# Attention, gated and softplus layers on one core: an operand sum moved into its PSUM bank

## The chip, the cores and the metric

One core of one Trainium2 chip runs the whole kernel as one program. The metric is device time in microseconds; a run's time is that of its one core. Before the change the median of 3 runs is 587.61 us (587.58 to 587.76).

## What is computed

The reference is attention with a learned distance bias, then a gated layer, then a softplus layer, all in fp32:

```python
scores = scale * q @ k.T + bias(heads, S, S)         # B=2, H=8, S=576, D=64
attn = softmax(scores) ; out = attn @ v               # -> x: 1152 tokens x 512
x = (silu(x @ w_gate) * (x @ w_val)) @ w_out          # 512 -> 1536 -> 512
x = softplus(x @ w_in) @ w_out2                       # 512 -> 2048 -> 512
```

The products of the layers take fp32 operands as two parts each: a high part (a rounded cast) and a low part (the value minus its high part). They also use a scheme with fewer products of 2 x 2 blocks (Strassen's, in Winograd's form). The attention output, turned so that features lie on partitions, is the right operand. Its four blocks are called B11, B12, B21 and B22, and the scheme needs sums of them: T1 = B12 - B11, T2 = B22 - T1, T3 = B22 - B12, T4 = T2 - B21 up to sign. Each sum must exist as a high part and a low part before the gated layer starts at about 186 us.

## The kernel before, in words

The attention stage is written out slot by slot. A unit is a pair of heads of one batch; `UNITS` (L495) lists eight of them. Each unit is done in two halves of its rows: sub 0 has 4 chunks and 256 columns, sub 1 has 5 chunks (one of them, "mix", takes both heads) and 320 columns. `run_slot` (L521) handles one chunk, and PE, VectorE (DVE), ScalarE (ACT), GpSimd (POOL) and SP each execute in the order in which this code issues, since the whole stage stands under a manual schedule (L594). In a slot the order is:

1. the chunk's scores on PE (L333, into `ps`, of which there are two buffers),
2. for a half whose value products ended in the slot before, `finish` (L440) is made, a generator whose steps are spread over slots; in the code before it is only appended here (L553 to L557),
3. `gather` (L408): copies of transposed weights from PSUM, mostly on ACT,
4. `biased` (L342, DVE L354): scores plus bias into SBUF and the row minimum; it frees `ps`,
5. `softmax` (L366) of the chunk before: exp on ACT (L368), and at the end of a batch a reduce and a reciprocal on DVE (L372, L375) and scalings on POOL (L378),
6. two steps of `prep`: high parts of the next unit's k and q on DVE or ACT (L189, L191), low parts on POOL or DVE (L195). One of four low parts of k is DVE's, three are POOL's,
7. `advance(late)` (L568): the next step of each `finish`,
8. transposes on PE (L405) and, when a half's last piece is gathered, all its value products (L432) into `po`, a PSUM bank of which there is one. Then `advance(waiting)` (L586) runs the steps that waited for the next half's products.

So a score buffer is free for the scores of chunk n+2 when `biased` of chunk n is done. "The first chunk behind" a half's products is called n1 below, the next ones n2, n3 and so on.

The name B12 is reached four times: in units 1 and 3, in both halves. Called **A** (unit 1, sub 0), **B** (unit 1, sub 1), **C** (unit 3, sub 0) and **D** (unit 3, sub 1) here, their products end at about 72.9, 92.4, 114.6 and 123.6 us. Before, `finish` does there (L462 to L473): in n1's step 7 an ACT copy `po` to `b12` and DVE `t1f = po - B11h`; at the end of the next half's products DVE `t1f -= B11l` (SBUF); one slot later ACT T1h, a cast of `t1f`; at the end of the products behind that (one half later still for sub 1) DVE T1l = `t1f` - T1h (SBUF). `t1f` and `b12` lie in a dead part of `bias1`, so the trace calls them bias. All subtractions of `minus` show as line L452. Units 4 and 5 make B22 and read `t1f` and `b12` (L474 to L478).

Of the kernel before, what the change touches and what calls it, by code (L numbers as in the profile page):

```python
# [44 lines left out]
BLOCK = "block"  # L45
# [58 lines left out]
def tile_kernel(ctx: ExitStack, tc, qT, kT, vS, vT, wg, wv, wo, wi, wo2, table, out):  # L104
    nc = tc.nc
# [11 lines left out]
    def slots(pool, tag, names):  # L117

        for name in names:
            n = len([1 for t in SLOTS.values() if t[0] == tag])  # L120
            SLOTS[name] = (tag, [pool.tile([P, 2, S], F32R, tag=f"{tag}{2 * n + i}", name=f"{name}{t}") for i, t in enumerate("hl")])

    def opener(stack):
        return lambda name, bufs, **k: stack.enter_context(
            tc.tile_pool(name=name, bufs=bufs, reuse_waits="tile", **k)
        )

    rctx = ExitStack()
    with ExitStack() as actx:
# [38 lines left out]
        def load_k(i):  # L168
            pr, b = UNITS[i]
            kr = kp.tile([P, 2, S], F32, tag="kst", name="kr") if i < PLAIN else bias[0][:, :2]  # L170
            load(kr, kT, pr, b)
            return dict(i=i, pr=pr, b=b, kr=kr)

        def load_q(u):
            u["qr"] = early[7] if u["i"] == 1 else qraw.tile([P, 2, S], F32, tag="qr", name="qr")
            load(u["qr"], qT, u["pr"], u["b"])

        def load_v(u):
            pr, b = u["pr"], u["b"]
            v = u["v"] = vp.tile([P, 4, 3 * D], F32, name="v")  # L180
            vt = u["vt"] = vts[u["i"] % 3]
            sp.dma_start(out=v, in_=vS[b, pr].rearrange("p (c e) -> p c e", c=4))
            thirds = lambda ap: ap.rearrange("p (t e) -> p t e", t=3)
            sp.dma_start(out=thirds(vt[:D])[:, ::2], in_=thirds(vT[b, pr])[:, ::2])
            sp.dma_start(out=vt[D:, D : 2 * D], in_=vT[b, pr, :, D : 2 * D])
# [254 lines left out]
        def finish(u):  # L440

            if u["i"] == 2 and u["sub"] == 0:
                slots(xp, "a", ("B21", "B22"))
            if u["i"] == 4 and u["sub"] == 0:
                right.close()
                SLOTS["rp8"] = (None, opener(rctx)("rp8", 1, side="right"))
                slots(SLOTS["rp8"][1], "r", ("T2", "T3", "T4"))
            pr, sub, po = u["pr"], u["sub"], u["po"]
            n = 320 if sub else 256
            cols = slice(256 * sub, 256 * sub + n)  # L450
            po = po[:, :n]
            minus = lambda o, a, b, eng=nc.vector: eng.tensor_tensor(o, a, b, op=ALU.subtract)  # L452
            at = lambda name: [t[:, pr % 2, cols] for t in SLOTS[name][1]]
            floats = lambda name: [t.bitcast(F32) for t in at(name)]
            name = f"B{1 + pr // 2}{1 + u['b']}"
            if name != "B12":
                nc.scalar.copy(at(name)[0], po)
            k = pr % 2
            home = bias[1][:, 2 * k : 2 * k + 2, cols]
            t1f, b12 = home[:, 0], home[:, 1]  # L460
            chains = []
            if name == "B12":  # L462
                nc.scalar.copy(b12, po)
                minus(t1f, po, floats("B11")[0])
                yield BLOCK
                minus(t1f, t1f, floats("B11")[1])
                yield
                nc.scalar.copy(at("T1")[0], t1f)
                yield BLOCK
                if sub:  # L470
                    yield BLOCK
                minus(at("T1")[1], t1f, floats("T1")[0])
                return  # L473
            elif name == "B22":  # L474
                t2, t3 = t2f[:, k, cols], tmpp.tile([P, 320], F32, name="t")[:, :n]
                minus(t2, po, t1f)
                minus(t3, po, b12)
                chains = [("T2", t2), ("T3", t3)]  # L478
            elif name == "B21":
                t4 = tmpp.tile([P, 320], F32, name="t")[:, :n]  # L480
                minus(t4, po, t2f[:, k, cols])
                chains = [("T4", t4)]
            if not u["eager"]:
                yield
            if name != "B12":
                minus(at(name)[1], po, floats(name)[0])
            if u["eager"]:
                yield
                yield
            for to, t in chains:  # L490
                nc.scalar.copy(at(to)[0], t)
                yield
                minus(at(to)[1], t, floats(to)[0], nc.vector if u["eager"] else nc.gpsimd)
# [27 lines left out]
        def run_slot():  # L521
            nonlocal turned, done, prep, before, slot
            if slot < len(chunks):
                i, sub, n = chunks[slot]
                if n == 0:
                    for _ in prep:
                        pass
                    if (i, sub) == (1, 0):
                        load_v(units[1])
                    elif (i, sub) == (0, 1):  # L530
                        units.append(load_k(2))
                    elif sub and i + 1 < 2 * NP:
                        load_q(units[i + 1])
                        if i > 1:
                            load_v(units[i + 1])
                        prep = itertools.chain(prepare_k(units[i + 1]), prepare_q(units[i + 1], 0))
                    elif i > 1 and not sub:
                        if i + 1 < 2 * NP:
                            units.append(load_k(i + 1))
                        if i == 2:  # L540
                            load_v(units[2])
                            units[2][0].update(v=units[2]["v"], vt=units[2]["vt"])
                        prep = prepare_q(units[i], 1)
                    if i < PLAIN:
                        job(units[i], sub)
                    if i == NP and sub == 0:
                        flat = lambda ap: ap.rearrange("p a s -> p (a s)")
                        pairs[2:] = [flat(bias[c][:, 2 * a : 2 * a + 2]) for a in range(2) for c in (2, 3)]
                        mixes[1] = flat(bias[4][:, :2])[:, : 5 * P]
                        nc.gpsimd.memset(mixes[1][:, S:], 0.0)  # L550
                u = units[i][sub]
                got = scores(u, n)
            for w in done:  # L553
                w["eager"] = slot >= len(chunks) - 1
                late.append(finish(w))
                if w["eager"]:
                    next(late[-1])  # L557
            done = []
            for w, piece, got_t in turned:
                gather(w, piece, *got_t)  # L560
            if slot < len(chunks):
                biased(u, n, *got)
            if before:
                softmax(*before)
                before = None
            for _ in range(2):
                next(prep, None)
            advance(late)  # L568
            held, turned = [t[:2] for t in turned], []

            over = slot >= len(chunks)
            for _ in range(2 if slot % 9 in TWICE or over else 1):
                if jobs and jobs[0][2] <= slot:
                    w, piece, _ = jobs.pop(0)
                    turned.append([w, piece, transposes(w, piece, over and (piece == "f" or next(spare)))])
            gathered.extend(held)

            ends = [i + 1 for i, (w, piece) in enumerate(gathered) if piece == PIECES[w["sub"]][-1]]
            last_job = over and gathered and gathered[0][0] is units[-1][1]
            for _ in range(len(gathered) if last_job else max(ends, default=0)):  # L580
                w, piece = gathered.pop(0)
                values(w, piece)
                if piece == PIECES[w["sub"]][-1]:
                    done.append(w)
            if done:
                advance(waiting)  # L586
            if slot < len(chunks):
                before = (u, n)
                if n == 3 + sub:
                    jobs.extend((u, piece, slot + LAG) for piece in PIECES[sub])  # L590
            slot += 1
# [125 lines left out]
    class Quad:  # L717
# [8 lines left out]
        def floats(self):  # L726
            self.x = as_float(self.n)
# [129 lines left out]
    with tc.manual_schedule(engines={E.PE}):  # L857
# [118 lines left out]
        for m, order in ((2, (0, 1, 2)), (3, (2, 0, 1))):  # L976
            pt = [wide()[:, 0] for _ in TB]
            for fbs in [order[:1], order[1:]] if m == 3 else [(fb,) for fb in order]:
                at = {fb: blocks.index((m, fb)) for fb in fbs}
                ws = {fb: convert(NL1 + 3 + i // 2)[i % 2] for fb, i in at.items()}  # L980
                for ps, (o, n) in reversed(list(zip(pt, TB))):
                    for fb in fbs:
                        part = lambda k: [g[NK * fb + k][:, o : o + n] for g in (gh, gl)]
# [167 lines left out]
```

## Time and profile before

| | us |
|---|---|
| median of 3 runs (lowest, highest) | 587.61 (587.58, 587.76) |
| profiled execution: span from first to last instruction | 585.8 |
| median less span (what lies around the span) | 1.8 |
| attention stage behind the bias, its value products and sums | about 63 to 186 |
| PE, DVE, ACT, POOL busy in the span | 575.7, 454.2, 374.8, 98.4 |

The page has no time of the profiled execution beyond its span; the 1.8 us is the difference to the median of the runs shown. PE's granted clock is at its upper level in every slice. A busy PE is not PE at its peak, since the ends of matmuls are modelled, so the distance between the same two steps of the PE order in different places is the better measure of a stall. In the rows below a start is in us from the span's start, "x4" is a count of merged instructions, and a bracket gives the idle time before an instruction and what ended it.

### The profile page before, as it was taken

The page shows a single profiled execution, that of the slowest core. Times are in us where ns is not written, and L with a number is a line of the kernel's source. Part 1 is how long each engine was busy: PE and PEld are TensorE (multiplying, and loading weights), DVE is VectorE, ACT ScalarE, POOL GpSimd, SP SyncE. Part 2 cuts the span into 40 slices and gives each one's busy share as a digit, 9 for nine tenths or more (in the row PEclk, how much of TensorE's full clock was granted, in tenths as well). Part 3 has the DMA queues.
Part 4 walks back from the last instruction along what each step waited for, and adds up shares of the span by engine and source line. Part 5 has one row for each costly group of instructions (what it writes and reads, how often), then busy time and mean ns, then how long its engine had stood idle before and what let it go on. Part 6 is the DMA issues. An engine that isn't in the chain of part 4 may idle for free.

```text
span 585.8 us, 11304 instructions
## 1 busy us (share of the span) xinstructions
PE 575.7 (98%) x4270; PEld 506.2 (86%) x4270; DVE 454.2 (78%) x970; ACT 374.8 (64%) x713; POOL 98.4 (17%) x151
## 2 busy tenths in 40 slices
PE   8999999999999999999999999999999999999997
PEld 5334588888887999999999999999989989989985
DVE  7999688888988998977879626579998877974332
ACT  8999888888787857656568325359727715733610
POOL 1002578888861000000000000000000000000000
PEclk9999999999999999999999999999999999999999
DMA  8999633233233342332343231322243241300012
GB/s 312 208 208 221 153 94 128 81 107 112 72 115 113 99 143 74 108 109 73 108 130 124 75 113 46 106 94 73 83 162 117 73 143 38 108 36 1 2 62 99
DMA packets 41894, 63.30 MB, mean 108 GB/s; under 512 B 4080, under 2 KB 30704, under 8 KB 41840
## 3 DMA queue, kind: packets, MB, share of 16 engines
q1 hardware_dynamic: 41840, 62.59, 36.1%
q8 instruction: 33, 0.54, 0.4%
q14 instruction: 21, 0.17, 0.1%
HBM read 49.60 MB, written 2.36 MB: 89 GB/s over the span
## 4 chain that ended last, share of the span: by engine, by line
PE 83%; DVE 7%; ACT 5%; DMA 3%; POOL 1%; issue 1%; DVEq 0%; ACTq 0%; POOLq 0%
PE pw L751 38%; PE pw L1059 17%; PE pw L702 13%; PE po L432 5%; PE pt L405 4%; PE ps L333 4%; DMA bias<-early 2%; PE ps L306 2%; ACT r L260 1%; PE pb L270 1%; ACT early L282 1%; DVE e L354 1%; DVE r L262 1%; DVE bias L354 1%; DVE T1l L452 1%
## 5 line engine op out<-in xcount | busy, mean ns | idle before, releaser
L1059 PE MATMUL pw<-oh,g2h 128*128 128x512 f32 x144 | 56.2, 390 | 0.0
L1059 PE MATMUL pw<-oh,g2l 128*128 128x512 f32 x144 | 56.2, 390 | 0.0
L1059 PE MATMUL pw<-ol,g2h 128*128 128x512 f32 x144 | 56.1, 390 | 0.0
L702 PE MATMUL pw<-gl,sh 128*128 128x384 f32 x144 | 48.2, 335 | 0.0
L702 PE MATMUL pw<-gh,sl 128*128 128x384 f32 x144 | 48.2, 334 | 0.0
L702 PE MATMUL pw<-gh,sh 128*128 128x384 f32 x144 | 48.2, 334 | 0.0
L262 DVE TENSOR_SCALAR r<-G 128x576 f32<-128x576 f32 x108 | 47.2, 522 | 0.1
L676 DVE SCALAR_TENSOR_TENSOR x<-raw,x 128x512 int32<-128x512 int32 x68 | 46.3, 688 | 0.9
L270 PE MATMUL pb<-r,G 128*32 128x288 f32 x576 | 44.4, 414 | 2.1
L378 POOL TENSOR_SCALAR e<-e,sm 128x576 f32<-128x576 f32 x44 | 33.8, 776 | 65.7 <-DVE sm L375 59.2
L270 PEld LDWEIGHTS pb<-r,G 128*32 128x32 f32 x576 | 18.8, 110 | 26.8 <-ACT early L282 15.1
L354 DVE CUSTOM_DVE_ANT_0 e<-ps,bias 128x576 f32<-128x576 f32 x44 | 33.0, 750 | 11.4 <-PE ps L333 6.6
L412 ACT COPY at<-pt 128x512 f32<-128x512 f32 (+2 forms) x69 | 36.4, 548 | 6.5 <-PE pt L405 6.1
L333 PE MATMUL ps<-kst,ql 128*128 128x288 f32 x120 | 36.9, 336 | 1.4 <-DVE sm L372 0.7
L432 PE MATMUL po<-at,v 128*64 128x256 f32 (+3 forms) x384 | 37.3, 332 | 1.0 <-DVE at L412 0.8
L1097 DVE TENSOR_TENSOR acc<-pw,acc 128x512 f32<-128x512 f32 x27 | 17.5, 685 | 25.1 <-PE pw L1059 25.1
L368 ACT ACTIVATE e<-e,sm 128x576 f32<-128x576 f32 x44 | 34.3, 781 | 3.5 <-DVE sm L354 3.0
L673 DVE TENSOR_SCALAR x<-x 128x512 int32<-128x512 int32 x68 | 28.8, 428 | 9.7 <-ACT x L672 5.0
L432 PEld LDWEIGHTS po<-at,v 128*64 128x64 f32 x384 | 26.8, 137 | 8.5 <-issue 1.7
L1059 PEld LDWEIGHTS pw<-oh,g2l 128*128 128x128 f32 x144 | 27.0, 188 | 5.8
L333 PE MATMUL ps<-kst,qh 128*128 128x288 f32 x120 | 32.0, 295 | 0.0
L681 ACT CAST oh<-x 128x512 fp32r<-128x512 f32 x16 | 9.9, 619 | 34.1 <-PE pw L1059 33.7
(270 smaller groups left out, 1684.3 us busy)
## 6 DMA issues: line engine op xcount, KB each, us to landing
raw<-in_wo_dram SPq DMA_DIRECT2D x28, 512.0 KB, 3.4
bias<-early SPq DMA_DIRECT2D x32, 288.0 KB, 8.1
raw<-in_wi_dram SPq DMA_DIRECT2D x16, 512.0 KB, 4.1
raw<-in_wv_dram SPq DMA_DIRECT2D x12, 512.0 KB, 4.6
raw<-in_wg_dram SPq DMA_DIRECT2D x12, 512.0 KB, 3.5
qr<-in_qT_dram SPq DMA_DIRECT2D x7, 576.0 KB, 3.7
bias<-in_kT_dram SPq DMA_DIRECT2D x6, 576.0 KB, 4.4
v<-in_vS_dram SPq DMA_DIRECT2D x8, 384.0 KB, 3.2
```

The lines of the kernel that those rows point to most:

```text
L262: nc.vector.tensor_scalar(r, G[:, w0 : w0 + S], PB[:, n : n + 1], 0.0, op0=ALU.add, op1=ALU.max)
L270: nc.tensor.matmul(pb[32 * ct : 32 * ct + 32, hf, :HALF], W2, rs[ct][:, HALF * hf : HALF * (hf + 1)], start=True, stop=True,)
L333: nc.tensor.matmul(ps[:, hf, :HALF], u[t][:, o : o + P], kst[:, a, HALF * hf : HALF * (hf + 1)], start=i == 0, stop=i == len(parts) - 1,)
L354: nc.vector.tensor_tensor_reduce(out=e[:, :S].rearrange("p (a n) -> p a n", a=2), in0=ps[:, :, :HALF], in1=bt.rearrange("p (a n) -> p a n" ...
L368: nc.scalar.activation(e, e, AF.Exp, bias=sm[:, 0, n : n + 1], scale=-1.0, accum_out=u["sums"][:, n, :1])
L378: nc.gpsimd.tensor_scalar(e, e, sm[:, 2, i : i + 1], 1.0, op0=ALU.mult, op1=ALU.mult)
L412: marks[eng, u["i"], u["sub"]] = copy(at[:, :w], pt[:, :w]).ins
L432: nc.tensor.matmul(u["po"][D * a : D * (a + 1), o : o + n], v[:, D * t : D * (t + 1)], at[:, i : i + n], start=piece == 0 and o == 0, stop ...
L676: nc.vector.scalar_tensor_tensor(yi, lw, 29, yi, op0=ALU.logical_shift_right, op1=ALU.bitwise_or)
L702: nc.tensor.matmul(ps[:, :n], w[:, k], x, start=first and k == 0 and i == 0, stop=last and k == NK - 1 and i == 2)
L751: nc.tensor.matmul(ps[:, hf, :HALF], a[:, o + k], b[:, HALF * hf : HALF * (hf + 1)], start=start and k == 0 and i == 0, stop=k == 1 and i ...
L1059: nc.tensor.matmul(ps, g, w.rearrange("p k f -> p (k f)"), start=f == 0 and i == 0, stop=f == 3 and i == 2)
```

## The change

At the four places, four steps stand at the head of n1's slot, ahead of its gathers, its `biased` and its exp: the ACT copy `po` to `b12`, both subtractions on DVE (now in place, `po` - B11h and then `po` - B11l, PSUM to PSUM) and the ACT cast T1h from `po`. In step 7 of the same slot ACT copies `po` to `t1f`, and DVE makes T1l from `po` and T1h. Nothing is left for later slots.

```diff
             if name == "B12":
                 nc.scalar.copy(b12, po)
-                minus(t1f, po, floats("B11")[0])
-                yield BLOCK
-                minus(t1f, t1f, floats("B11")[1])
+                for part in floats("B11"):
+                    minus(po, po, part)
+                nc.scalar.copy(at("T1")[0], po)
                 yield
-                nc.scalar.copy(at("T1")[0], t1f)
-                yield BLOCK
-                if sub:
-                    yield BLOCK
-                minus(at("T1")[1], t1f, floats("T1")[0])
+                nc.scalar.copy(t1f, po)
+                minus(at("T1")[1], po, floats("T1")[0])
                 return
...
                 late.append(finish(w))
-                if w["eager"]:
+                if w["eager"] or (w["pr"] < 2 and w["b"]):
                     next(late[-1])
```

## Rows read from the trace of the kernel before

**Rows 1.** The page: the chain that ended last, share of the span by engine

```profile
PE 83%; DVE 7%; ACT 5%; DMA 3%; POOL 1%; issue 1%; DVEq 0%; ACTq 0%; POOLq 0%
```

**Rows 2.** Timeline of PE: start, length, line, matmuls; n4's scores at B, ends of stretches

```profile
95.52 0.38 PE L333 MATMUL ps<-kst,ql 128*128 128x288 f32 x1
...
114.64 0.40 PE L333 MATMUL ps<-kst,ql 128*128 128x288 f32 x1
...
120.52 2.45 PE L432 MATMUL po<-at,v 128*64 128x320 f32 x31
...
139.83 0.40 PE L333 MATMUL ps<-kst,ql 128*128 128x288 f32 x1
...
145.21 1.95 PE L432 MATMUL po<-at,v 128*64 128x256 f32 x16
...
147.51 0.40 PE L333 MATMUL ps<-kst,ql 128*128 128x288 f32 x1
...
155.10 2.45 PE L432 MATMUL po<-at,v 128*64 128x320 f32 x31
...
158.13 0.40 PE L333 MATMUL ps<-kst,ql 128*128 128x288 f32 x1
...
162.69 1.95 PE L432 MATMUL po<-at,v 128*64 128x256 f32 x16
```

**Rows 3.** Line L452, by operands: count, least/median/greatest ns, first and last start

```profile
L452 DVE TENSOR_TENSOR bias<-po,B11h x4: 404/444/470, 74.7 to 125.3; 128x256 f32<-128x256 f32 x2, 128x320 f32<-128x320 f32 x2
L452 DVE TENSOR_TENSOR bias<-bias,B11l x4: 406/790/1159, 81.5 to 130.0; 128x256 f32<-128x256 f32 x2, 128x320 f32<-128x320 f32 x2
L452 DVE TENSOR_TENSOR T1l<-bias,T1h x4: 411/636/3404, 91.6 to 146.6; 128x256 fp32r<-128x256 f32 x2, 128x320 fp32r<-128x320 f32 x2
```

**Rows 4.** Timeline of DVE at place B, behind C and behind D

```profile
93.21 0.76 DVE L354 CUSTOM_DVE_ANT_0 e<-ps,bias 128x576 f32<-128x576 f32 x1 [1.15 <-PE ps L333]
...
93.89 0.15 DVE L372 TENSOR_REDUCE sm<-sums 128x2 f32<-128x4 f32 x1
...
94.62 0.76 DVE L354 CUSTOM_DVE_ANT_0 e<-ps,bias 128x576 f32<-128x576 f32 x1
...
119.64 0.65 DVE L195 TENSOR_TENSOR kst<-bias,kst 64x288 fp32r<-64x288 f32 x1 [0.50 <-ACT kst L189]
...
135.79 1.70 DVE L195 TENSOR_TENSOR kst<-bias,kst 64x288 fp32r<-64x288 f32 x1 [0.74 <-ACT kst L189]
...
146.57 3.40 DVE L452 TENSOR_TENSOR T1l<-bias,T1h 128x320 fp32r<-128x320 f32 x1
```

**Rows 5.** Timeline of POOL around the same steps

```profile
119.16 2.54 POOL L195 TENSOR_TENSOR kst<-bias,kst 64x288 fp32r<-64x288 f32 x3
...
134.74 2.43 POOL L195 TENSOR_TENSOR kst<-bias,kst 64x288 fp32r<-64x288 f32 x3
...
146.39 0.74 POOL L378 TENSOR_SCALAR e<-e,sm 128x576 f32<-128x576 f32 x1
...
148.76 0.87 POOL L452 TENSOR_TENSOR T3l<-t,T3h 128x320 fp32r<-128x320 f32 x1
```

**Rows 6.** Timeline of ACT at place B, and the T1h cast of place D

```profile
91.18 0.57 ACT L412 COPY at<-pt 128x512 f32<-128x512 f32 x1
91.64 0.78 ACT L368 ACTIVATE e<-e,sm 128x576 f32<-128x576 f32 x1
92.32 0.19 ACT L368 ACTIVATION_READ_ACCUMULATOR e<-e,sm 128x1 f32 x1
92.48 0.42 ACT L463 COPY bias<-po 128x320 f32<-128x320 f32 x1
...
131.17 0.46 ACT L468 CAST T1h<-bias 128x320 fp32r<-128x320 f32 x1 [0.43 <-DVE bias L452]
```

**Rows 7.** The chain of waits, in order of time: scores of n1 and n4 at B

```profile
92.44 0.73 PE ps L333 x4
...
95.76 0.53 PE ps L333 x4
```

## The prediction

> **What bounds the kernel now.** I read the page first: PE is busy for nearly the whole span (the table above), and the chain that ended last is 83% PE and 7% DVE [rows 1]. A busy PE doesn't show a stall here, so the second view was PE's timeline, read as distances between equal steps of its order. From n1's scores behind one half's products to the next half's products there are 5.88 us (114.64 to 120.52) behind C's sub 0 products, but 7.59 us (147.51 to 155.10) for the same kind of stretch 33 us later; for the other kind 4.56 us (158.13 to 162.69), but 5.38 us (139.83 to 145.21) [rows 2]. So PE sets the pace through most of the attention stage and loses time in two stretches between 136 and 152 us. The third view, DVE's timeline, says to what: T1l of place D at 146.57 lasts 3.40 us, and the low part of k at 135.79 lasts 1.70 us where 0.65 us is usual [rows 4]. The fourth, POOL's timeline, shows why: the 3.40 us lie under four POOL instructions in a row, from 146.39 to 149.63 (the first and the last are shown), and the 1.70 us under POOL's three low parts of k, from 134.74 [rows 5]. All the stretched subtractions read two SBUF operands: the four T1l go from 411 to 3404 ns, the four `t1f -= B11l` from 406 to 1159 ns, while those from `po` stay within 404 to 470 ns [rows 3].
>
> **What it takes away.** (1) T1l of D at 146.57 goes; made from `po` it has one SBUF operand, so 0.47 us by its kind [rows 3], and it is made at 125 to 130 us. DVE gets back 3.40 us there. PE gets at most 7.59 - 5.88 = 1.71 us; I take 1.45, since in this stretch DVE also forms T2 and T3. (2) The cast T1h of D on ACT, with its wait (0.43 + 0.46 us [rows 6]), goes from 131.17, ahead of the exps and of k's high part, which releases the low part at 135.79. That one then asks up to 0.4 to 0.9 us earlier, while POOL's first subtraction runs (2.43 / 3 = 0.81 us each, from 134.74 [rows 5]), as it does at 119.64 (0.48 us behind POOL's start, 0.65 us long [rows 4, 5]). PE's gain is 5.38 - 4.56 = 0.82 us in the stretch behind, and up to the 1.05 us by which the low part shrinks in the products before it, which wait for DVE's next gather; I take 1.35 of at most 1.87, and 0 if the phase stays. (3) The other T1l, the four `t1f -= B11l` and the other three T1h leave places where DVE or ACT has slack before the next scores. Nothing is gained; DVE's count of subtractions is the same (three per place).
>
> **What it adds: a chain at the head of n1.** All queues are in order, and every step needs the one before: the in-place subtraction must wait for the copy that reads the same bank, T1h for the second subtraction. What stands behind on ACT is n1's gather and the exp of the chunk before; behind that exp's sum DVE has a reduce and a reciprocal, then T1l, then `biased` of n2; and n4's scores wait for that score buffer. Place B in numbers (steps from rows, 0.03 us between engines):
> - products end 92.44 [rows 7]; ACT `b12` from 92.50, 0.42 us [rows 6], to 92.92. In the kernel before, ACT does the gather (91.18) and the exp (91.64) while PE still multiplies [rows 6]; now both stand behind this.
> - DVE subtracts twice, 0.47 us each [rows 3], to 93.42 and 93.92.
> - ACT T1h, 0.46 us [rows 6], to about 94.40; gather, 0.46 us from start to start; exp from 94.8 instead of 91.64; its sum is there 0.87 us later (0.68 + 0.19) [rows 6], at 95.67.
> - DVE `biased` of n1 runs from 93.9 instead of 93.21 [rows 4], hidden beside that. The reduce takes 0.15 us [rows 4], the reciprocal is taken as long, 0.35 us with the gaps (an estimate from that row); T1l 0.39 us from start to start: `biased` of n2 starts at 96.44 instead of 94.62 [rows 4], 1.82 us late, and ends at 97.2.
> - n4's scores began at 95.52 by the timeline, 95.76 by the chain [rows 2, 7], right behind the end of that `biased` (95.38). So they come 1.5 to 1.7 us late. I take **1.6 us**, and PE has nothing else to do in its order.
>
> D has B's width and order: 1.6 us. C has 256 columns, four steps shorter by some 0.07 us, but a cast of k's high part behind: 1.5 us. A has 256 columns and no gather ahead of its exp, so about 1.07 us of delay, and more distance to n4: between 0 and 1.1, taken as 0.3. One thing more at C: k's high part on ACT comes almost 2 us late, POOL's low parts only about 1.4 (they wait for DVE), so DVE's low part asks about 1.0 us behind POOL's start, the phase of the stretched one (135.79 - 134.74 = 1.05 [rows 4, 5]). It costs 0 to 1.05 us on DVE; I take 0.5 on PE.
>
> **Unknown price.** No row has DVE writing PSUM. From below it is the 0.40 us of the same subtraction into SBUF [rows 3]; from above the 0.65 us of an ordinary low part of k with its wait [rows 4]. I take 0.47 us, the nearest row in operands and width; the upper end adds about 0.2 us for each of two steps at three places, 1.2 us. The extra ACT copy `t1f` (0.42 us [rows 6]) lies beside the reduce; were it not hidden it would cost 0.4 us a place. The head removes nothing from PE, SP or POOL.
>
> **Sum.** Loss 0.3 + 1.6 + 1.5 + 1.6 + 0.5 = 5.5 us; gain 1.45 + 1.35 = 2.8 us; +2.7 us. The layers behind are PE's own work, so the shift passes to the end. The span of 585.8 becomes 588.5; with the 1.8 us to the median, 587.6 becomes **590.3 us**.
>
> **Rivals.**
> - *The low part at C is let in.* In the trace, T1l at 146.57 asked during one POOL instruction and was held through three more [rows 4, 5]. The Trainium skill (SBUF — State Buffer, "Who interferes with whom") says that the one that issues first has the shared ports for its whole instruction and the other is blocked; by that rule the wait should have ended with the first of the four, at 147.13, and the trace disagrees by 2.5 us. As a mechanism of this kernel: if the request at C is granted when POOL's running subtraction ends, the 0.5 us go, +2.2 us, 589.8 us. For it: the request at 119.64 is granted so. Against: 135.79 isn't.
> - *The low part at 135.79 stays stretched.* PE's loss at D shifts POOL and ACT together, and their phase is decided by tenths. Then 1.35 us aren't gained: 591.65 us.
> - *The head is mostly hidden.* `biased` of n2 would come in time for n4: its 1.82 us delay at B, C and D costs PE only a third, because the lag is caught in the 2.3 to 3 us of value products that follow. Loss 0.3 + 3 x 0.6 + 0.5 = 2.6 us against 2.8: 587.4 us. For it: DVE waits 1.15 us for PE at 93.21 [rows 4]. Against: n4 stands ahead of those products, and its buffer was free only 0.14 us before it was used.
> - *Faster.* The head's loss stays out of PE altogether, as when ACT's T1h at the head doesn't hold the gather and the exp. It decides at one point: whether `biased` of n2 at B starts before about 94.8. If so, only the gain is left: 587.6 - 2.8 = 584.8 us. Against it stands the order of issue, in which T1h is ahead of both on an in-order queue.
>
> **Chances.** 0.2% of this time is 1.2 us, about what a measurement of this kernel can tell from no change. Forecast 0.42, low part let in 0.17, low part stays stretched 0.15: slower 0.74. Mostly hidden: same 0.14. Faster 0.12. The forecast's own range is 588.9 to 591.5 (A and C at their bounds, then 1.2 us for the PSUM writes); the whole range, 588.2 to 591.9, takes in the stretched case and leaves out the hidden ones and the extremes of the PSUM price.
>
> **What would show it.** Right: at B, ACT `b12`, T1h, gather, exp in this order, exp near 94.8 and n4's scores 1.5 us later than before against the products' end; DVE subtractions from `po` into `po` near 0.47 us; no DVE subtraction above 1 us at T1; the stretch behind B22's first half back near 6.1 us. Wrong: n4's scores at B, C and D where they were; a stretch at 147 us that stays at 7.6 us; a subtraction into PSUM far from 0.47 us; or a low part of k that is stretched in another place and so turns the sum.

## The result and the profile after

| | before | after |
|---|---|---|
| median (lowest, highest), us | 587.61 (587.58, 587.76) | 591.36 (591.28, 591.72) |
| profiled execution: span, us | 585.8 | 589.5 |

The changed kernel takes 1.0062 times as long (95% interval 1.0051 to 1.0073): 3.75 us slower. The forecast was 590.3 us in a range of 588.2 to 591.9. The direction and the range held; the sum of +2.7 us was 1.05 us too small.

The page names no culprit. Busy times move by at most 4 us (DVE 454.2 to 450.3), and what stands out is the chain that ended last, in which ACT now has 7% (5% before) and DVE 3% (7% before, [rows 1]).

```profile
PE 575.9 (98%) x4270; PEld 504.0 (85%) x4270; DVE 450.3 (76%) x970; ACT 375.7 (64%) x717; POOL 97.2 (16%) x151
...
PE 86%; ACT 7%; DVE 3%; issue 2%; POOL 1%; POOLq 0%; ACTq 0%; DVEq 0%
```

So the time has to be found by distances. PE does the same work in the same order in both kernels, so I took the starts of successive halves' value products from PE's timeline and subtracted the distances. This ledger is used for every run below; a column is the stretch from one half's products to the next, named by the kernel before's times. Numbers are us against the kernel before; stretches not listed differ by at most 0.1 unless said. The medians come from several rounds of runs; in these the kernel before took 587.45 to 587.78 us, and each ratio below is to its runs of the same round.

| run | A 70–80 | B 89–97 | C 112–121 | D 121–128 | 128–136 | 136–145 | 145–155 | median |
|---|---|---|---|---|---|---|---|---|
| distance before | 9.55 | 7.32 | 8.19 | 7.32 | 8.42 | 8.95 | 9.89 | 587.61 |
| after | +1.19 | +1.75 | +1.45 | +1.77 | −0.07 | −1.37 | −1.01 | 591.36 |
| e1, T1h behind the yield | +0.68 | +0.57 | +0.36 | +0.56 | −0.06 | −1.37 | −1.04 | 587.38 |
| e2, no head | +0.09 | +0.40 | +0.30 | +0.41 | −0.07 | −1.36 | −1.04 | 586.32 |
| e5, no head, three slots | +0.96 | +2.37 | +1.97 | +2.39 | +1.43 | −0.72 | −1.49 | 594.87 |
| e4, before, D's T1l earlier | 0 | 0 | 0 | 0 | 0 | +0.30 | −1.47 | 586.58 |
| e3, before, with the head | +0.16 | +0.07 | +0.12 | +0.08 | +0.59 | −0.06 | −0.76 | 588.78 |
| e3b, the same kernel | +0.17 | +0.07 | +0.13 | +0.07 | +0.58 | 0 | 0 | 588.48 |
| e7, bank free in two slots | 0 | 0 | +0.16 | 0 | −0.06 | −1.37 | −1.02 | 585.35 |
| e8, T1l on DVE | 0 | 0 | +0.19 | 0 | −0.06 | −1.36 | −1.01 | 585.47 |
| e10, before, POOL freed | 0 | 0 | 0 | 0 | 0 | 0 | −0.97 | 586.76 |
| e12, after, T3 in place | +1.20 | +1.77 | +1.46 | +1.75 | −0.06 | −1.37 | −0.99 | 590.92 |
| e11, e7 with T3 in place | 0 | 0 | +0.18 | 0 | −0.05 | −1.36 | −1.04 | 585.06 |

After loses 1.19 + 1.75 + 1.45 + 1.77 = 6.16 us at the four places and gains 0.07 + 1.37 + 1.01 = 2.45 us behind them. The net 3.71 us agrees with the difference of the spans, 3.7. The change therefore has two halves that can be looked at apart.

**The loss, at place B.** The products end at 93.62 here. The chain of waits of after, for the stretch around B (start, length, what):

```profile
93.62 0.73 PE ps L333 x4
...
95.50 0.36 ACT at L412
...
95.98 0.89 ACT e L368 x2
...
97.70 0.67 DVE e L354
```

Before, nothing but PE's own steps lay between 92.44 and 95.76 [rows 7]. Here the chain leaves PE at the gather and comes back to PE's scores of n4 at 98.43, 4.81 us behind the products' end. Before, PE began the same scores at 95.52 [rows 2], 3.08 us behind it. (The chain before lists them at 95.76, because it counts a step of PE from the end of the one before it; the timeline's starts are the like measure.) So n4 comes 1.73 us late, which is nearly all of B's 1.75; the prediction took 1.5 to 1.7 from this chain. ACT's timeline of after at B shows why the gather is late:

```profile
93.66 0.43 ACT L463 COPY bias<-po 128x320 f32<-128x320 f32 x1 [1.20 <-PE po L432]
95.18 0.43 ACT L466 CAST T1h<-po 128x320 fp32r<-128x320 f32 x1 [1.10 <-DVE po L452]
95.50 0.59 ACT L412 COPY at<-pt 128x512 f32<-128x512 f32 x1
95.98 0.79 ACT L368 ACTIVATE e<-e,sm 128x576 f32<-128x576 f32 x1
```

In each bracket stands ACT's idle time. It idled 1.20 us for the products and then 1.10 us for DVE's two subtractions, while n1's gather and the exp, which needed neither, stood behind. The exp begins 2.36 us behind the products' end; before, it began ahead of it [rows 6]. DVE's timeline of after at B continues the chain:

```profile
94.11 0.50 DVE L452 TENSOR_TENSOR po<-po,B11h 128x320 f32<-128x320 f32 x1 [1.20 <-ACT bias L463]
94.65 0.50 DVE L452 TENSOR_TENSOR po<-po,B11l 128x320 f32<-128x320 f32 x1
95.06 0.75 DVE L354 CUSTOM_DVE_ANT_0 e<-ps,bias 128x576 f32<-128x576 f32 x1
...
96.89 0.16 DVE L372 TENSOR_REDUCE sm<-sums 128x2 f32<-128x4 f32 x1 [1.08 <-ACT e L368]
...
97.21 0.49 DVE L452 TENSOR_TENSOR T1l<-po,T1h 128x320 fp32r<-128x320 f32 x1
97.62 0.75 DVE L354 CUSTOM_DVE_ANT_0 e<-ps,bias 128x576 f32<-128x576 f32 x1
```

The last line is n2's `biased`, 4.00 us behind the products' end; before it was 94.62 − 92.44 = 2.18 behind [rows 4, 7], so 1.82 later, the prediction's own number. It isn't the only path from ACT to PE. PE's transposes also wait for late gathers (0.40 us at 96.15, 0.38 at 97.72; 2.1 us over the four places, a wait which the kernel before's list doesn't have), and behind them PE idles only 0.27 us more for `biased` before n4's scores. PE's timeline:

```profile
97.72 0.44 PE L405 MATMUL pt<-ident,e 128*128 128x128 f32 x2 [0.38 <-ACT at L412]
98.43 0.40 PE L333 MATMUL ps<-kst,ql 128*128 128x288 f32 x1 [0.27 <-DVE sm L354]
```

The gathers alone would have made n4 about 1.73 − 0.27 = 1.46 us late (an estimate from these rows). At C the chain of waits runs through them and not through `biased`:

```profile
120.81 0.61 ACT at L412
...
121.47 0.66 PE pt L405 x4
122.12 1.32 PE ps L333 x8
```

ACT's extra copy to `t1f` (120.56, 0.37 us), which the prediction took as hidden, stands just ahead of that gather. Both paths begin at the same place, ACT's queue behind T1h.

**The loss, at place A.** POOL's timeline of after, and under "..." PE's:

```profile
76.00 1.47 POOL L378 TENSOR_SCALAR e<-e,sm 128x576 f32<-128x576 f32 x2 [1.89 <-DVE sm L375]
77.43 1.46 POOL L195 TENSOR_TENSOR ql<-qr,qh 128x256 fp32r<-128x256 f32 x2
...
78.25 0.40 PE L333 MATMUL ps<-kst,ql 128*128 128x288 f32 x1 [1.15 <-POOL ql L195]
```

The late exp makes DVE's reciprocal late, POOL's scalings wait for that, and q's low part stands behind them on POOL. PE needs it for the next unit's first scores, which are n4's here, and waits 1.15 us. The same two steps in the kernel before:

```profile
76.24 1.46 POOL L195 TENSOR_TENSOR ql<-qr,qh 128x256 fp32r<-128x256 f32 x2
...
77.07 0.40 PE L333 MATMUL ps<-kst,ql 128*128 128x288 f32 x1
```

The products begin at 70.51 in both kernels, and the scalings began at 74.81 before; after, all three steps are 1.18 to 1.19 us later.

**The gain.** PE's timeline of after at the products and, under "...", DVE's two low parts of k that the prediction spoke of, C's and the one that was at 135.79:

```profile
133.98 1.95 PE L432 MATMUL po<-at,v 128*64 128x256 f32 x16
142.33 2.45 PE L432 MATMUL po<-at,v 128*64 128x320 f32 x31
149.91 1.95 PE L432 MATMUL po<-at,v 128*64 128x256 f32 x16
158.79 2.45 PE L432 MATMUL po<-at,v 128*64 128x320 f32 x31
...
124.50 0.46 DVE L195 TENSOR_TENSOR kst<-bias,kst 64x288 fp32r<-64x288 f32 x1 [0.83 <-ACT kst L189]
...
141.59 0.46 DVE L195 TENSOR_TENSOR kst<-bias,kst 64x288 fp32r<-64x288 f32 x1 [0.48 <-ACT kst L189]
```

The low part that lasted 1.70 us [rows 4] lasts 0.46, and its stretch is 149.91 − 142.33 = 7.58 us long instead of 8.95. T1l at 146.57 is gone; all L452 subtractions of T1, grouped by operands (least/median/greatest ns), are now short:

```profile
L452 DVE TENSOR_TENSOR po<-po,B11h x4: 432/466/500, 73.4 to 128.5; 128x256 f32<-128x256 f32 x2, 128x320 f32<-128x320 f32 x2
L452 DVE TENSOR_TENSOR po<-po,B11l x4: 432/466/499, 73.8 to 129.0; 128x256 f32<-128x256 f32 x2, 128x320 f32<-128x320 f32 x2
L452 DVE TENSOR_TENSOR T1l<-po,T1h x4: 412/452/490, 75.9 to 131.6; 128x256 fp32r<-128x256 f32 x2, 128x320 fp32r<-128x320 f32 x2
```

### The profile page after: what moved, and what is told of

The parts are those of the page before. It is cut to its first block, busy times and chain, and to the rows that moved or that the text cites. A ratio compares the mean times of both kernels' runs of the same rounds, so it can differ in the third digit from the quotient of the medians.

```text
span 589.5 us, 11306 instructions
## 1 busy us (share of the span) xinstructions
PE 575.9 (98%) x4270; PEld 504.0 (85%) x4270; DVE 450.3 (76%) x970; ACT 375.7 (64%) x717; POOL 97.2 (16%) x151
## 3 DMA queue, kind: packets, MB, share of 16 engines
HBM read 49.60 MB, written 2.36 MB: 88 GB/s over the span
## 4 chain that ended last, share of the span: by engine, by line
PE 86%; ACT 7%; DVE 3%; issue 2%; POOL 1%; POOLq 0%; ACTq 0%; DVEq 0%
PE pw L748 38%; PE pw L1056 17%; PE pw L699 13%; PE po L432 7%; PE ps L333 5%; PE pt L405 4%; ACT early L282 3%; PE pb L270 2%; ACT r L260 2%; PE ps L306 1%; ACT e L368 1%; PE warm L594 1%; DVE e L354 1%; POOL e L378 0%; ACT at L412 0%
## 5 line engine op out<-in xcount | busy, mean ns | idle before, releaser
L270 PEld LDWEIGHTS pb<-r,G 128*32 128x32 f32 x576 | 16.7, 110 | 28.9 <-ACT early L282 15.9
L405 PE MATMUL pt<-ident,e 128*128 128x128 f32 x188 | 32.0, 277 | 1.4 <-ACT at L412 1.3
```

The costliest lines, as they stand in the source:

```text
L270: nc.tensor.matmul(pb[32 * ct : 32 * ct + 32, hf, :HALF], W2, rs[ct][:, HALF * hf : HALF * (hf + 1)], start=True, stop=True,)
L405: nc.tensor.transpose(pt[:, P * w : P * (w + 1)], e, ident)
```

## The experiments

The theory: T1h on ACT, waiting at the head, costs most of the loss; the head and the second subtraction cost the rest; the gain comes from the T1l and the T1h that went away. The rivals: the in-place subtractions on DVE are the cost, or the head as such, or the gain is only a lucky phase of DVE against POOL.

**e1: T1h behind the yield** (ahead of step 7's copy instead of at the head).

```diff
                 for part in floats("B11"):
                     minus(po, po, part)
-                nc.scalar.copy(at("T1")[0], po)
                 yield
+                nc.scalar.copy(at("T1")[0], po)
                 nc.scalar.copy(t1f, po)
```

> As the changed kernel, but the cast T1h stands behind the yield: the copy to b12 and both subtractions stay at the head of n1, T1h comes in step 7 with the copy to t1f and T1l. Theory 1 (T1h at the head holds n1's gather and exp, and through the reduce the row step of n2 and n4's scores): the exp of n1 comes 1.3 to 1.5 us earlier at B, C and D, so the PE losses there fall from 1.75, 1.46 and 1.75 us to 0.1 to 0.4 each and at A from 1.19 to under 0.3; 2.4 us of gain stay; 586.0 us, within 585.5 to 587.0. Rival 1 (the head itself costs: the wait for the products and the pair of subtractions ahead of n1's row step): more than half of the 6.15 us stays, 588.5 us or more.

587.38 us, ratio 0.9996 (0.9988 to 1.0005) to the kernel before: the one cast's place costs 591.36 − 587.38 = 4.0 us of the 6.16. I had expected more of it back (585.5 to 587.0 us): the four places keep 0.36 to 0.68 us each. ACT's timeline of e1 at B, whose products end at 93.14:

```profile
93.17 0.43 ACT L463 COPY bias<-po 128x320 f32<-128x320 f32 x1 [1.20 <-PE po L432]
93.50 0.59 ACT L412 COPY at<-pt 128x512 f32<-128x512 f32 x1
93.97 0.79 ACT L368 ACTIVATE e<-e,sm 128x576 f32<-128x576 f32 x1
94.75 0.43 ACT L467 CAST T1h<-po 128x320 fp32r<-128x320 f32 x1
```

The wait of 1.10 us is gone. The same cast takes the same 0.43 us, but nothing waits for DVE ahead of the exp.

**e2: no head, two slots** (e1, and the second hunk of the diff undone, so that the pair runs in step 7).

```diff
-                if w["eager"] or (w["pr"] < 2 and w["b"]):
+                if w["eager"]:
```

> Nothing at the head: copy to b12 and both in-place subtractions in step 7 of n1, then T1h, copy to t1f and T1l in step 7 of n2. Theory 1: no exp or gather waits for a subtraction, the two stretched subtractions between two SBUF operands are gone all the same, so only the gain of 2.4 us is left, less 0.2 to 0.3 us at B, C and D where two subtractions instead of one stand ahead of n2's row step: 585.5 to 586.3 us. Rival 2 (forming the sum in PSUM, with its extra ACT copies, is what costs, wherever it stands): 588 us or more.

586.32 us, ratio 0.9978 (0.9969 to 0.9987), at the upper end of what I expected. The head, with everything a slot earlier, costs a further 1.06 us; e2 is faster than the kernel before. DVE's timeline of e2 at B shows what is left of the loss:

```profile
94.18 0.48 DVE L452 TENSOR_TENSOR po<-po,B11h 128x320 f32<-128x320 f32 x1
94.69 0.50 DVE L452 TENSOR_TENSOR po<-po,B11l 128x320 f32<-128x320 f32 x1
95.10 0.75 DVE L354 CUSTOM_DVE_ANT_0 e<-ps,bias 128x576 f32<-128x576 f32 x1
```

Two subtractions where there was one stand ahead of n2's `biased`, and B keeps 0.40 us.

**e5: no head, three slots** (the second subtraction and T1h one slot later still, T1l in n3).

```diff
                 nc.scalar.copy(b12, po)
-                for part in floats("B11"):
-                    minus(po, po, part)
+                minus(po, po, floats("B11")[0])
+                yield
+                minus(po, po, floats("B11")[1])
                 nc.scalar.copy(at("T1")[0], po)
                 yield
```

> Nothing at the head, and one subtraction a slot: copy to b12 and the first in-place subtraction in step 7 of n1, the second and T1h in n2, copy to t1f and T1l in n3. Theory 1: DVE has one subtraction in n1, as before the change, so no loss ahead of n4's scores: the gain of 2.4 us alone, 585.2 us, within 584.8 to 586.0; T1h waits on ACT for the second subtraction in n2 by some 0.3 us, which may cost part of it. Rival 2: 588 us or more.

A miss: 594.87 us, the slowest of all, ratio 1.013 (1.0115 to 1.0146). PE's waits in e5 (us in all, times, longest) and, under "...", its timeline behind B:

```profile
PE po L432 <- DVE T1l L452: 5.8, 3, 2.3
...
100.03 1.95 PE L432 MATMUL po<-at,v 128*64 128x256 f32 x16 [2.31 <-DVE T1l L452]
```

There is one bank `po`. As long as T1l reads it the next half's products can't start, and T1l had moved behind the slot in which they are due. Spreading steps out helps only up to that slot. e1 reads the bank in one slot and e2 in two, and neither has such a wait.

**e4: the kernel before, with T1l of sub 1 one half earlier.**

```diff
                 yield BLOCK
-                if sub:
-                    yield BLOCK
                 minus(at("T1")[1], t1f, floats("T1")[0])
```

> The kernel before, but T1l of sub 1 is made at the end of the next half's products instead of one half later (at B near 105 to 108 us, at D near 137 to 139 us instead of 146.6). It tells whether the gain comes from the stretched T1l of D at 146.57. Theory 1: the 3.40 us subtraction is not there any more and PE gets 1.0 to 1.5 us back, 586.1 to 586.6 us, unless it is stretched in its new place as well. Rival 3 (the stretched T1l costs PE nothing, the gain comes from elsewhere): 587.6 us, no change.

586.58 us, ratio 0.9982 (0.9973 to 0.9991). DVE's timeline of e4:

```profile
135.85 1.68 DVE L195 TENSOR_TENSOR kst<-bias,kst 64x288 fp32r<-64x288 f32 x1 [0.75 <-ACT kst L189]
...
140.32 0.49 DVE L452 TENSOR_TENSOR T1l<-bias,T1h 128x320 fp32r<-128x320 f32 x1
```

As expected. The same T1l with the same two SBUF operands takes 0.49 us at 140.32, although POOL is at work across it (two scalings from 139.50 to 141.35), and the stretch behind loses 1.47 us; in the stretch where it now stands 0.30 us are added. The low part of k stays at 1.68: the two gains are separate. That the second comes from T1h's leaving 131.17 is read from the traces. Behind the start of D's next products (127.84 before, 133.98 in after) the low part asks 0.34 us earlier in after, 7.61 for 7.95. No run moves that cast alone: in every version with the gain two DVE subtractions ahead of it (at 129.45 and 129.98 before) have left too. But e8 below has another DVE subtraction at that place (T1l, 0.68 us at 130.12), and the whole gain.

**e3 and e3b: the kernel before, with the head** (`b12` and the first subtraction at the head; one `yield` more, so that the steps behind stay in their slots). e3b is the same kernel again, one execution.

```diff
                 minus(t1f, po, floats("B11")[0])
+                yield
                 yield BLOCK
...
-                if w["eager"]:
+                if w["eager"] or (w["pr"] < 2 and w["b"]):
```

> The kernel before, with one thing of the change: the copy to b12 and the first subtraction (into SBUF, as before) stand at the head of n1, ahead of its gather, row step and exp; all that follows is spread as before. It prices the head without T1h and without a sum in PSUM. From the run without a head against the one with T1h behind the yield (586.32 and 587.38 us) the head's place alone should cost about 1.0 us, most of it at A, where q's low part on POOL comes later: 588.2 to 589.0 us. If the head costs only through T1h: 587.6 us. If a head of any kind costs as in the changed kernel: 590 us or more.

> The same kernel as the one before with a head, looked at once more: its profiled execution lay 0.8 us under the median of its runs (587.98 against 588.78), so the profile shows only 0.4 us of the head's 1.0 us. If the kernel takes one of two courses through the attention stage, a second profile near the median shows a further 0.6 to 0.9 us at one place, by the distances between value products: at the stretched subtraction of D or at a low part of k, where DVE and POOL meet (theory 1), or at A, B, C and D alike (the head's own cost, spread).

The head alone costs about 1 us, but not where I expected it (most at A): A has 0.16 and 0.17, and 0.58 lies in the stretch behind D. e3b's trace says how it gets there. ACT's late exp at D holds DVE's reduce for 0.85 us (0.20 before); DVE stays behind against the products from there on, its row step at 133.53 by 0.59 us, and PE's scores at 134.34 wait for it. So it is D's own cost, paid one stretch later. e3's runs spread over 587.98 to 589.25. L452's T1l group in the two traces, e3 first:

```profile
L452 DVE TENSOR_TENSOR T1l<-bias,T1h x4: 409/638/675, 91.9 to 148.3; 128x256 fp32r<-128x256 f32 x2, 128x320 fp32r<-128x320 f32 x2
```

```profile
L452 DVE TENSOR_TENSOR T1l<-bias,T1h x4: 408/640/3406, 91.7 to 147.5; 128x256 fp32r<-128x256 f32 x2, 128x320 fp32r<-128x320 f32 x2
```

In two executions of one kernel the longest T1l is 675 ns and 3406 ns, and the stretch from 145 to 155 follows it: −0.76 and 0. So the 3.40 us of [rows 4] depend on small shifts, not on the code alone. In both the longest is D's, and POOL runs the same scaling of `e` and then `ql` as it asks: in e3 it asks 0.41 us behind that scaling's start, in e3b 0.19.

**e7 and e8: bank free in two slots.** No head; the first subtraction in place in n1, the second out of the bank into SBUF in n2, the cast and T1l in the slots behind it, from SBUF. e7 has T1l on POOL, e8 on DVE. The diff is against the changed kernel, without the hunk for the head.

```diff
                 nc.scalar.copy(b12, po)
-                for part in floats("B11"):
-                    minus(po, po, part)
-                nc.scalar.copy(at("T1")[0], po)
+                minus(po, po, floats("B11")[0])
                 yield
-                nc.scalar.copy(t1f, po)
-                minus(at("T1")[1], po, floats("T1")[0])
+                minus(t1f, po, floats("B11")[1])
+                yield
+                nc.scalar.copy(at("T1")[0], t1f)
+                yield
+                minus(at("T1")[1], t1f, floats("T1")[0], nc.gpsimd)
```

> Nothing at the head. n1: copy to b12 and the first subtraction in place; n2: the second subtraction, from PSUM into t1f, after which the bank is free; n3: T1h from t1f; n4: T1l on POOL. DVE has one subtraction ahead of n2's row step, as before the change, and none with two SBUF operands. If the 1.1 us that the two-slot version loses at B, C and D are its second subtraction ahead of n2: 585.2 us, within 584.7 to 585.8. The bank is let go in n2, when the next products want it within 0.2 us, so no wait like the three-slot version's 2.3 us is expected. If POOL's four extra subtractions (0.75 to 0.9 us each) delay q's low parts: up to 586.5 us.

> As the run with T1l on POOL, but T1l stays on DVE, with two SBUF operands (t1f and T1h), in n4. Whether it is stretched is decided by what POOL does just then: without a stretch 585.0 to 585.5 us; with one of 1 us or more at C or D, where POOL's low parts of k and scalings run back to back, 585.8 to 587 us.

585.35 us (ratio 0.9958, 0.9946 to 0.9971) and 585.47 us (0.996, 0.9947 to 0.9972), both as expected and faster than either kernel. The four places cost 0 to 0.19 us and the gain of after is whole: the loss isn't the price of the gain. L452 in e7, and then e8's T1l:

```profile
L452 DVE TENSOR_TENSOR po<-po,B11h x4: 410/453/480, 74.6 to 125.4; 128x256 f32<-128x256 f32 x2, 128x320 f32<-128x320 f32 x2
L452 DVE TENSOR_TENSOR bias<-po,B11l x4: 405/441/484, 76.2 to 127.3; 128x256 f32<-128x256 f32 x2, 128x320 f32<-128x320 f32 x2
...
L452 POOL TENSOR_TENSOR T1l<-bias,T1h x4: 730/804/876, 81.1 to 131.0; 128x256 fp32r<-128x256 f32 x2, 128x320 fp32r<-128x320 f32 x2
```

```profile
L452 DVE TENSOR_TENSOR T1l<-bias,T1h x4: 417/546/677, 79.5 to 130.1; 128x256 fp32r<-128x256 f32 x2, 128x320 fp32r<-128x320 f32 x2
```

e8's T1l still has two SBUF operands, but asks where POOL holds it 0.2 us at most. POOL's longer T1l in e7 costs nothing, because nobody waits for it.

**e10: the kernel before, with T2's and T3's low parts of unit 4's second half on DVE instead of POOL.**

```diff
-                minus(at(to)[1], t, floats(to)[0], nc.vector if u["eager"] else nc.gpsimd)
+                minus(at(to)[1], t, floats(to)[0], nc.vector if u["eager"] or (u["i"], sub) == (4, 1) else nc.gpsimd)
```

> The kernel before, but T2l and T3l of unit 4's second half are made on DVE instead of POOL, so that only two POOL instructions, not four, stand in a row over T1l of D. If that subtraction was held by POOL's back-to-back run: 1.4 to 2.0 us long instead of 3.40, ending about 0.3 us behind POOL's second instruction; the time within 0.5 us of before, since DVE has two subtractions more. If it was held by something else (its operands, the bank, its own form): 3.4 us still. If only one POOL instruction ever holds it: about 1.0 us, but that was so before as well and didn't hold.

586.76 us, ratio 0.9983 (0.9974 to 0.9992), 1.0 us from the kernel before where I expected at most 0.5; the stretch loses 0.97 us although DVE has two subtractions more. DVE's timeline of e10, and under the last "..." POOL's:

```profile
147.49 1.20 DVE L452 TENSOR_TENSOR T3l<-t,T3h 128x320 fp32r<-128x320 f32 x1
148.61 0.48 DVE L452 TENSOR_TENSOR T1l<-bias,T1h 128x320 fp32r<-128x320 f32 x1
...
147.47 0.87 POOL L195 TENSOR_TENSOR ql<-qr,qh 128x320 fp32r<-128x320 f32 x1
```

T3l asks 0.02 us behind POOL's start, ends 0.35 us behind POOL's end, and T1l, beside an idle POOL (its next step is at 150.21), takes 0.48 us, not the 1.4 to 2.0 that I expected. So with POOL idle the stretch of T1l is gone; but the test isn't quite clean, since T3l now stands in T1l's place.

**e12 and e11: T3 in its own place.** In after the stretch from 145 to 155 gained 1.01 us, not 1.45. Its traces held a candidate, DVE's timeline and then POOL's:

```profile
154.83 0.42 DVE L452 TENSOR_TENSOR t<-po,bias 128x256 f32<-128x256 f32 x1 [0.42 <-POOL T3l L452]
...
153.91 0.89 POOL L452 TENSOR_TENSOR T3l<-t,T3h 128x320 fp32r<-128x320 f32 x1
```

Both halves of B22 use one buffer `t`: DVE may not write the next half's T3 until POOL has read the last one's. Before, DVE was held until 149.90 anyhow. e12 is after and e11 is e7, each with T3 formed in the place of `b12`.

```diff
-                t2, t3 = t2f[:, k, cols], tmpp.tile([P, 320], F32, name="t")[:, :n]
+                t2, t3 = t2f[:, k, cols], b12
```

> The changed kernel, with the float of T3 formed in place of `b12` instead of in the one buffer `t` that both halves share. Theory (the gain behind D was 1.01 us and not the 1.45 forecast because DVE's write of `t` at 154.83 waited 0.42 us for POOL's T3l of the half before, which still read `t`): the wait goes, the stretch between the value products from 145 to 155 us becomes 0.4 us shorter than in the changed kernel (about -1.45 against the kernel before), the places A to D stay as they are (+1.2, +1.75, +1.45, +1.75), median about 590.9 us; a little more if the second wait of this kind, behind unit 5's halves, also costs PE something. Rival (the 0.42 us lie beside other work, and the rest of the gain was lost to something else, such as POOL's later scalings): the stretch stays at -1.0, median 591.3 us. A second rival: the subtraction po - b12 in place has two operands that touch one SBUF place and is slower than 0.42 us, which would show at T3.

> The same edit on the fastest version so far (no head, bank free in two slots, T1l on POOL; 585.35 us). Theory: 0.4 us from the stretch behind the first half of B22, 584.9 us or a little less (the trace of that version shows the same wait for POOL's T3l twice, 1.0 us in all). Rival: 585.3 us, no change.

The medians are near what the theory said, 590.92 us (ratio 1.0055, 1.0041 to 1.0068) and 585.06 us (584.74 to 585.26; ratio 0.9954, 0.9942 to 0.9967), yet the ledger says that it is wrong about this stretch: −0.99 and −1.04. The 0.44 and 0.29 us by which they lie below after and e7 can come from later: the stretches from 163 to 171 and from 176 to 182 shrink by 0.3 and 0.1 us, of which the first held after's second wait of this kind (0.56 us at 171.13, ahead of T4's `t`). The spans of the two profiled executions don't show it (589.5 us in e12 and in after, 583.4 for 583.5 in e11 and e7), since PE's steps ahead of 63 us and behind 182 took 0.3 to 0.5 us longer in them. DVE's timeline of e12:

```profile
154.44 0.41 DVE L452 TENSOR_TENSOR bias<-po,bias 128x256 f32<-128x256 f32 x1
...
155.70 0.98 DVE L191 CAST kst<-bias 128x576 fp32r<-128x576 f32 x1
```

The wait is gone, and `po` - `b12` in place is no slower for it (0.41 us, the second rival). But DVE's cast of k, 0.45 us long in after, takes 0.98 here, beside POOL's scalings: the wait removed turned into a hold of about the same size. The intervals of e11 and e7 overlap, and so do those of e12 and after; that either is the faster of its pair isn't shown.

## Why the prediction was right and where it was wrong

- **Terms B, C and D** (1.6, 1.5, 1.6): right in size, measured +1.75, +1.45, +1.77. At B and D it is the chain that was worked out (at B the exp 2.36 us behind the products' end, n2's `biased` 1.82 us late, n4's scores 1.73 late). The second path, gathers and PE's transposes, wasn't counted; it is nearly as long, and at C it is the one in the chain of waits, so that C's size came out right by a path that the prediction hadn't priced. e1 shows that T1h's place, from which both paths start, is the main part of the loss.
- **Term A** (taken as 0.3, at most 1.1): wrong, and the step that failed. It measured 1.19 us. The delay of the reciprocal was as expected (1.19 us for 1.07); but the prediction followed it only to DVE's `biased` and n4's score buffer, where there was slack, and not to POOL, which also waits for that reciprocal and makes q's low part behind it. The kernel before had shown it without a bracket: the first scores with the new q began 0.83 us behind POOL's start on it, and 0.82 after, so there was no slack.
- **The low part at C** (0.5): didn't come. It asked 0.80 us behind POOL's start (124.50 − 123.70), not 1.0, and took 0.46 us. So the rival "the low part at C is let in" was right in its mechanism, though not with its 589.8 us. Judged by the time alone, 591.36 would have spoken for the rival in which the low part at 135.79 stays stretched (591.65); its row, 0.46 us at 141.59, rules that out.
- **The gain by that low part** (1.35): right, 1.37, and the same within 0.01 in after, e1, e2, e7, e8, e11 and e12, in all of which T1h has left that place. In after it asks 0.79 us behind POOL's start, just as POOL's first subtraction ends: 0.26 us earlier than before, where the prediction had 0.4 to 0.9.
- **The gain by T1l** (1.45): measured 1.01. e4 got 1.47 from the same removal, so the size was possible; in after and e7, which had gained 1.37 us just before, POOL was behind relative to PE (T3l starts 4.00 us behind the products' start in after, 3.55 in e4), and DVE waited for it or was held by it (after 0.42 for `t` and 0.78 for the low part of k behind, against 0 and 0.46 in e4). That this is the whole difference is argued from the two traces; e12, which took one of the waits away, got nothing back in this stretch.
- **The price of an in-place subtraction** (0.47): right, 0.466 in the median, 22 ns above the same subtraction into SBUF (0.444, the first group of [rows 3]). The upper bound of 0.65 is out.
- **The range.** It doesn't follow from its own bounds: A from 0 to 1.1 us and C's low part from 0 to 1.05 us give 589.5 to 591.65 us, and 1.2 us for the PSUM writes 592.85. The measured time lies in either range.
- **The sum.** From +2.7: A +0.89, B and D +0.32, C with its low part −0.55, T1l +0.44, the rest −0.09 give +3.7.

On contention the runs go further than the prediction. L452's subtractions on DVE with one SBUF operand stay within 402 to 500 ns in every run here; the long ones all have two. The Trainium skill (SBUF — State Buffer, "Who interferes with whom") says that a DVE instruction with at most one SBUF input does not contend with GpSimd outside the two-port modes, and that casts can enter those. The traces fit both (e12's cast, 0.98 for 0.45 us), though no trace shows a cast's mode. The Trainium skill's same page ("Summary: rules for kernel authors") has the second of the two to issue wait until the first finishes. e10 looks so (T3l ends just behind POOL's `ql`); the 3.40 us beside four POOL instructions don't, and e3's 675 ns against 3406 ns show that the same pair of queues does both.

The thirteen traces show what goes with the one and the other: how far into a POOL instruction the subtraction asks. Between 62 and 180 us, 129 DVE subtractions with two SBUF operands begin while POOL is at work. Of these, 88 begin 0.32 us or more behind the start of POOL's instruction; none of them is held past the end of that one, and the longest takes 0.88 us. Seven are held past it, 1.68 to 3.41 us long, and all seven begin 0.17 to 0.19 us behind its start with another POOL instruction right behind it. The two long subtractions of [rows 4] are among them. In after, the low parts at 124.50 and 141.59 begin 0.80 and 0.79 us behind it. One more, in e2, began 0.15 us behind in the same situation and was not held past. So the phase of 1.05 us, which the prediction counted from the start of POOL's group of three, is 0.17 us behind the instruction that then ran, and the traces go by the second number. Why they do no run here shows.

## What to carry to other kernels

An instruction moved to the head of an in-order queue costs the wait of everything behind it, not its own length: T1h is 0.37 to 0.43 us long, four times, and its place at the head cost 4.0 us against step 7 of the same slot. Look for every path from that queue to the bottleneck: relieving DVE's `biased` alone would have given back about 0.27 us at B (an estimate from PE's wait there). When a step is delayed, follow each engine that waits for it, POOL too, and take equal distances for "no slack" even where no wait is printed. Spread the steps of a chain over slots, but let the last reader of a single PSUM bank come ahead of the next use: e7 (two slots) is 2.4 us faster than the kernel before, e5 (three) 7.2 us slower.

## What the runs showed of the hardware that was not expected

- A DVE subtraction with two SBUF operands beside back-to-back POOL work took 675 ns in one execution and 3406 ns in the other of one and the same kernel; with one SBUF operand none of L452's took more than 500 ns. It asked 0.41 us behind the start of a POOL instruction in the first and 0.19 in the second; of 88 subtractions with two SBUF operands that asked 0.32 us or more behind, none was held past that instruction.
- DVE subtracts in place in PSUM, 128x256 and 128x320, in 432 to 500 ns (410 to 480 in e7), hardly more than into SBUF.
- Taking away a hold moves the next one: 0.42 us of waiting for POOL became 0.53 us of a slower cast (e12).
